# Opening of a spectral filter plus gated MLP kernel: column 0 in feature halves, first weights on ScalarE's queue, column 1 transposed inside the first up unit

## The chip, the cores and the metric

The kernel runs on one NeuronCore of a Trainium2 chip. The metric is the device time of one execution in microseconds (us); a time given for a kernel is the median of several runs. Traces come from one profiled execution, and times in them are counted from the start of its span.

## The reference

The input x has 2048 rows of 512 features (bfloat16). It is layer-normalized, and two branches of the normalized rows are added to x: a spectral filter (2-D real FFT, product with a complex weight, inverse FFT) and a gated MLP with 1792 hidden features.

```python
def _A_ref(x, w_r, w_i):
    X = rfft2(x.astype(float32), axes=(-2, -1))
    X = X * (w_r + 1j * w_i)
    return irfft2(X, s=(S, D), axes=(-2, -1)).astype(bfloat16)

def _B_ref(x, w_gate, w_up, w_down):
    g = einsum("bsd,df->bsf", x, w_gate)
    u = einsum("bsd,df->bsf", x, w_up)
    h = _gelu(g) * u                      # tanh form of gelu
    return einsum("bsf,fd->bsd", h, w_down)

xn = _layernorm(x, axis=-1)               # eps 1e-5
return x + _A_ref(xn, A_w_r, A_w_i) + _B_ref(xn, B_w_gate, B_w_up, B_w_down)
```

## The kernel before, in words

Row 16·p + c of x lies in partition p, column c. So x is held as 16 columns of 128 rows by 512 features (`x_t`), and "column c" below always means such a block. Each column is normalized into `xn` and transposed into `xnT`, four blocks of 128 features (e = 0 to 3) by rows, because the matmuls contract over features.

The MLP is cut into units. A unit takes n columns and m blocks of 128 hidden features (f): matmuls with `Wg_sb` into the PSUM tile `g_ps`, matmuls with `Wu_sb` into `u_ps`, a GELU on ScalarE from `g_ps` to `ge`, and on VectorE the product of `u_ps` and `ge` into `hT`. `g_ps` and `u_ps` have two buffers each; a GELU frees one of the first, a product one of the second. The first units are small, so that the work can begin when a single column is there: unit 0 is column 0 with f 0 to 3, unit 1 column 1 with f 0 to 3, units 2 and 3 are columns 0 and 1 with f 4 and 5 and with f 6 and 7; the next four take columns 2 and 3, and then come units of four columns and one f. The `todo` list has them in this order. The spectral branch (`forward`, `group`, `inverse`) and the down projection (`down`) fill the rest of the program.

The order on every engine is written out ahead. `opening()` emits the first memsets, the loads and 37 matmuls on zeros (`spin`), which keep TensorE busy until data come. All else is added to a `Plan` as operations with an engine, an assumed occupancy and latency, dependencies, a key and, for what needs a load, an assumed earliest time (`LAND`, `WG_LAND`, `WU_LAND`). `Plan.order()` simulates the engines with these numbers and emits the operations in the order it finds; the chip then keeps that order on each engine, and real waits come from semaphores. A changed assumption can therefore move operations anywhere in the program.

`first_two()` (line 372) plans columns 0 and 1. For column 0: moments on VectorE (L337), aggregate (L340), square root on ScalarE (L392), reciprocal (L397), normalization in two halves of 256 features (L343), four transposes on TensorE (L349), two copies of `tp` into `xnT` on ScalarE (L352), and in between six more spin matmuls (L322). For column 1 the same, with the normalization, the four transposes and the one copy (VectorE) undivided; the transposes stand in the key order after unit 0 and ahead of unit 1. The entry named `table` stands for the change of ScalarE's function table from Sqrt to GELU; it emits nothing, and the load itself is put in by the compiler ahead of the first GELU. `second_two()` plans columns 2 and 3 with their square roots on POOL (`root_eps`), and `later_four()` the others, which are transposed by DMA.

Unit 0 is emitted through `mm_half` (line 488), which runs e = 0, 1 over all four f and then e = 2, 3, so that it may begin with half of `xnT`. All other units use `mm` (line 480), which finishes one f after the other.

The loads are issued in program order by two queues, SyncE (SP) and ScalarE. A load takes one of eight semaphores in turn, and waits for the load that had it before.

Of the kernel before, what the change touches and what calls it, by code (L numbers as in the profile page):

```python
# [10 lines left out]
P = 128  # L11
BF16 = mybir.dt.bfloat16
F32 = mybir.dt.float32
# [4 lines left out]
S = 2048  # L18
D = 512
NC = 16  # L20
NG = 8
NE = 4
# [112 lines left out]
class Plan:  # L135
# [66 lines left out]
def kernel(  # L202
# [11 lines left out]
    nc = tc.nc  # L214
# [5 lines left out]
    x_v = A_x.rearrange("b (p c) d -> p c (b d)", c=NC)  # L220
# [7 lines left out]
    pw = ctx.enter_context(tc.tile_pool(name="pw", bufs=2))  # L228

    x_t = pc.tile([P, NC, D], BF16, name="x_t", tag="x_t")  # L230
    CT = pc.tile([P, const_np.shape[1]], BF16, name="CT")
    Wg_sb = pc.tile([P, NE, DF], BF16, name="Wg_sb")
    Wu_sb = pc.tile([P, NE, DF], BF16, name="Wu_sb")
# [19 lines left out]
    def load_x(c0, n, eng=nc.sync):  # L253
        eng.dma_start(out=x_t[:, c0:c0 + n, :], in_=x_v[:, c0:c0 + n, :])

    def load_w(a, b, eng=nc.sync):
        nc.sync.dma_start(out=Wg_sb[:, :, a:b], in_=wg_v[:, :, a:b])
        eng.dma_start(out=Wu_sb[:, :, a:b], in_=wu_v[:, :, a:b])
# [15 lines left out]
    def opening():  # L274
        nc.vector.memset(spin[:], 0.0)
        nc.vector.memset(eps_t[:], EPS)
        nc.vector.memset(minus_half[:], -0.5)
        U = nc.gpsimd
        U.memset(ident_t[:], 1.0)
        U.affine_select(out=ident_t[:], in_=ident_t[:], pattern=[[-1, P]], compare_op=ALU.is_equal, fill=0.0,  # L280
                        base=0, channel_multiplier=1)
        nc.scalar.activation(out=warm[:], in_=eps_t[:], func=AF.Sqrt, bias=eps_t[:], scale=1.0)
        load_x(0, 1)
        load_x(1, 1)
        load_w(Wg_sb, 0, 512, nc.scalar, e=slice(0, 2))
        load_w(Wg_sb, 0, 512, nc.scalar, e=slice(2, 4))
        for e in range(NE):
            load_w(Wu_sb, 0, 512, e=e)
        load_x(2, 2)
        load_w(Wg_sb, 512, 1024)  # L290
        load_w(Wu_sb, 512, 1024)
        load_x(4, 4)
        load_w(Wg_sb, 1024, DF)
        load_w(Wu_sb, 1024, DF)
        load_x(8, 4)
        nc.sync.dma_start(out=RF_t[:], in_=rf_d.rearrange("p (c k) -> p c k", c=NC))
        load_x(12, 4)
        nc.sync.dma_start(out=idx_t[:], in_=nc.inline_tensor(idx_np, name="spec_rows").ap())
        load_consts("F0", "L0")
        load_consts("I0", "M0")  # L300
        for T, w_in in ((TR, A_w_r), (TI, A_w_i)):
            rows = w_in.rearrange("(kb a h g) k -> h kb a (g k)", kb=NC, h=2, a=8)
            Tf = T.rearrange("p j k -> p (j k)")
            for h in range(2):
                nc.sync.dma_start(out=Tf[64 * h:64 * h + 64, W:8 * W], in_=rows[h, :, 0:4, W:8 * W])
        for k in range(37):
            nc.tensor.matmul(sp_ps[:, :P], lhsT=spin[:], rhs=spin[:], start=True, stop=True)  # L307

    LAND = {0: 2.9, 1: 4.5, 2: 7.2, 3: 7.2}
    LAND.update({c: 11.5 if c < 8 else 17.5 if c < 12 else 20.5 for c in range(4, NC)})  # L310
    WG_LAND = [5.0] * 4 + [8.6] * 4 + [13.2] * 6
    WU_LAND = [6.7] * 4 + [10.0] * 4 + [15.2] * 6
    RF_LAND = 19.0

    ident = ident_t[:]
# [23 lines left out]
    def f_mean(c):  # L339
        V.bn_aggr(out=mv[:, c, :], in_=tiles["st", c][:])  # L340

    def f_norm_v(c, o, w):
        V.tensor_scalar(out=xn[:, c, o:o + w], in0=x_t[:, c, o:o + w], scalar1=mv[:, c, 0:1],  # L343
                        scalar2=rstd[:, c:c + 1], op0=ALU.subtract, op1=ALU.mult)

    def f_T(c, e0, n):
        tiles["T", c, e0] = tp = ps.tile([P, n, P], BF16, name="tp", tag="S", bufs=4)
        for e in range(n):
            T_.transpose(tp[:, e], xn[:, c, (e0 + e) * P:(e0 + e + 1) * P], ident)  # L349

    def f_Tc(c, e0, n, copy=V.tensor_copy):
        copy(out=xnT[0][:, e0:e0 + n, c, :], in_=tiles["T", c, e0][:])  # L352
# [14 lines left out]
        U.tensor_tensor(out=b, in0=mv[:, c0:c0 + n, 0], in1=rstd[:, c0:c0 + n], op=ALU.mult)  # L367
        U.tensor_scalar(out=b, in0=b, scalar1=-1.0, scalar2=None, op0=ALU.mult)  # L368

    xn_op, xT_op = {}, {}  # L370

    def first_two():
        o = {}

        def v(k, fn, occ, deps=(), lat=None, t_min=0.0):
            o[k] = add("DVE", occ, fn, [o[d] for d in deps], key=-2000 + len(o), lat=lat, t_min=t_min,
                       after=o.get("last"))
            o["last"] = o[k]

        def T(c, h):  # L380
            o["T", c, h] = add("PE", 0.12, lambda: f_T(c, 2 * h, 2), [o["xn", c, h]], key=-2000 + 2 * c + h,
                               lat=0.36, acq=("S",))

        def xn_(c, h):
            v(("xn", c, h), lambda: f_norm_v(c, 256 * h, 256), 0.27, [("recip", c)], lat=0.4)

        def stats(c):
            v(("stats", c), lambda: f_stats(c), 0.6, t_min=LAND[c], lat=0.7)

        def mean(c):  # L390
            v(("mean", c), lambda: f_mean(c), 0.17, [("stats", c)])
            o["root", c] = add("ACT", 0.31, lambda: A.activation(  # L392
                out=rstd[:, c:c + 1], in_=mv[:, c, 1:2], func=AF.Sqrt, bias=eps_t[:], scale=1.0),
                [o["mean", c]], key=-2000 + c)

        def recip(c):
            v(("recip", c), lambda: V.reciprocal(out=rstd[:, c:c + 1], in_=rstd[:, c:c + 1]), 0.15, [("root", c)])  # L397

        stats(0)
        mean(0)  # L400
        recip(0)
        xn_(0, 0)
        xn_(0, 1)
        stats(1)
        mean(1)
        T(0, 0)
        T(0, 1)
        add("PE", 0.33, spin_on, [o["T", 0, 1]], key=-1500, lat=0.33, after=o["T", 0, 1])
        table = add("ACT", 1.3, lambda: None, [o["root", 1]], key=-1500, lat=1.3)
        xT_op[0, 0], xT_op[0] = (  # L410
            add("ACT", 0.36, lambda h=h: f_Tc(0, 2 * h, 2, A.copy), [o["T", 0, h]], key=-1990 + h, lat=0.48,
                rel=("S",)) for h in range(2))
        recip(1)
        xn_op[0] = o["xn", 0, 1]
        v("xn1", lambda: f_norm_v(1, 0, D), 0.33, [("recip", 1)], lat=0.45)
        t = add("PE", 0.23, lambda: f_T(1, 0, NE), [o["xn1"]], key=-1998, lat=0.45, acq=("S",))
        o["t"] = t
        v("copyt", lambda: f_Tc(1, 0, NE), 0.5, ["t"])
        o["copyt"].rel = ("S",)
        xT_op[1] = o["copyt"]  # L420
        xn_op[1] = o["xn1"]
        return o["copyt"]

    ROOT = 1.1
    chain_end = first_two()
# [39 lines left out]
    def unit(k, c0, n, f0, m=1):  # L465
# [19 lines left out]
                    T_.matmul(b[name][:, f], lhsT=W_[:, e, (f0 + f) * P:(f0 + f + 1) * P], rhs=rhs[:, e, :],  # L485
                              start=(e == 0), stop=(e == NE - 1))

        def mm_half(s, name="g_ps", tag="G", W_=Wg_sb):
            if s == 0:
                b[name] = ps.tile([P, m, w], F32, name=name, tag=tag, bufs=2)  # L490
            for e in (2 * s, 2 * s + 1):
                for f in range(m):
                    T_.matmul(b[name][:, f], lhsT=W_[:, e, (f0 + f) * P:(f0 + f + 1) * P], rhs=rhs[:, e, :],  # L493
                              start=(e + f == 0), stop=(e == NE - 1), skip_group_check=True)
# [12 lines left out]
        def split(name, tag, W_, key, t, h):  # L507
            o = None
            for f in range(0, m, h):
                o = add("PE", occ * h / m, lambda f=f: mm(name, tag, W_, range(f, f + h)), [o] if f else src, key=key,  # L510
                        lat=occ * h / m + 0.3, acq=() if f else (tag,), t_min=t[f0 + f + h - 1])
            return o

        if k == 0:
            g = add("PE", occ / 2, lambda: mm_half(0), [xT_op[0, 0]], key=1000, acq=("G",), t_min=WG_LAND[0])
            g = add("PE", occ / 2, lambda: mm_half(1), [xT_op[0], g], key=1000.1, lat=occ / 2 + 0.3)
            u = add("PE", occ / 2, lambda: mm_half(0, "u_ps", "U", Wu_sb), [g], key=1000.5, acq=("U",), t_min=6.2)
            u = add("PE", occ / 2, lambda: mm_half(1, "u_ps", "U", Wu_sb), [u], key=1000.6, lat=occ / 2 + 0.3,
                    t_min=WU_LAND[0])
        else:  # L520
            g = split("g_ps", "G", Wg_sb, 1000 + k, WG_LAND, m)
            u = split("u_ps", "U", Wu_sb, 1000.5 + k, WU_LAND, (2, m, 1)[k] if k < 3 else m)
        ge = add("ACT", {1: 0.28, 2: 0.36, 4: 0.5}[n * m], f_ge, [g], key=-1000 + k,
                 lat={1: 0.38, 2: 0.48, 4: 0.7}[n * m], acq=("ge",), rel=("G",))
        h = add("DVE", {1: 0.21, 2: 0.34, 4: 0.61}[n * m], f_h, [ge, u], key=-1000 + k, rel=("U", "ge"))
# [354 lines left out]
```

## Time and profile before

| | us |
|---|---|
| median of four runs | 178.89 |
| their lowest and highest | 178.69, 180.44 |
| the profiled execution | 179.09 |
| its span | 177.4 |
| TensorE busy in the span | 172.1 |
| first matmul of unit 0, of unit 1 | 6.07, 9.23 |
| first transpose of columns 2 and 3 | 12.76 |

In lines of the profile, PE is TensorE's matmul side, PEld its weight loads, DVE is VectorE, ACT is ScalarE, POOL is GpSimd, SP is SyncE. A name such as SPq or ACTq is the issue of a DMA by that engine. `L485` is line 485 of the kernel. A bracket at the end of a line tells how long the engine had been idle and what ended it. In a line of waits the numbers are the total, the count and the longest wait.

### The profile page before, as it was taken

Reading aid. Unit: us, or ns where it says so; the run is one execution under the profiler, and the core shown is the slowest. Engines: PE = TensorE matmul, PEld = TensorE weight load, DVE = VectorE, ACT = ScalarE, POOL = GpSimd, SP = SyncE. Lnnn points to the kernel's source line nnn. Section 1 sums busy time; section 2 is a strip of 40 time slices with the busy share of each in tenths; the row PEclk is TensorE's granted clock in tenths of the full one; section 3 lists DMA queues with packets and bytes.
Section 4 is the critical chain, followed back from the end, with each engine's and each line's share of the span. In section 5 each row is a group of like instructions: output and inputs, shape, how many; then the busy total and the mean of one; then the engine's idle time right before and its main releaser. Section 6 shows DMA issues by size and latency. Waiting matters only on the chain.

```text
span 177.4 us, 3114 instructions
## 1 busy us (share of the span) xinstructions
PE 172.1 (97%) x1128; PEld 97.5 (55%) x1145; DVE 115.6 (65%) x253; ACT 96.4 (54%) x172; POOL 17.0 (10%) x38
## 2 busy tenths in 40 slices
PE   7999999999999999999999999999999999999993
PEld 7888845464545554555555545454445444444463
DVE  2488899988333599998799999543526334344333
ACT  4623489798745989799999955453112111211200
POOL 1020360406760000000000000000000000000000
PEclk9999999999999999999999999999999999999999
DMA  5999986543718702121202520200132221221212
GB/s 149 324 368 393 349 168 99 111 91 56 240 33 265 267 4 59 36 53 35 59 10 49 142 72 0 59 0 4 53 95 89 70 81 61 89 86 62 78 44 59
DMA packets 21360, 19.35 MB, mean 109 GB/s; under 512 B 8481, under 2 KB 20001, under 8 KB 21345
## 3 DMA queue, kind: packets, MB, share of 16 engines
q1 hardware_dynamic: 20384, 17.31, 33.8%
q0 software_dynamic: 416, 1.32, 2.6%
q10 hardware_dynamic: 544, 0.52, 1.1%
q8 instruction: 9, 0.15, 0.4%
q14 instruction: 7, 0.05, 0.1%
HBM read 13.38 MB, written 2.10 MB: 87 GB/s over the span
## 4 chain that ended last, share of the span: by engine, by line
PE 97%; issue 1%; DVE 1%
PE u_ps L485 27%; PE y_ps L815 27%; PE g_ps L485 26%; PE sp_ps L307 2%; PE yp L766 2%; PE dp L633 2%; PE gp L736 2%; PE bp L575 2%; PE y_ps L819 2%; PE ep L642 2%; PE g_ps L493 1%; PE tp L349 1%; PE u_ps L493 1%; PE sp_ps L322 0%; DVE xnT L352 0%
## 5 line engine op out<-in xcount | busy, mean ns | idle before, releaser
L485 PE MATMUL u_ps<-xnT,Wu_sb 128*128 128x512 bf16 (+2 forms) x254 | 56.5, 349 | 0.3
L485 PE MATMUL g_ps<-xnT,Wg_sb 128*128 128x512 bf16 (+2 forms) x246 | 55.2, 348 | 0.8 <-DVE xnT L352 0.5
L503 DVE TENSOR_TENSOR hT<-u_ps,ge 128x512 bf16<-128x512 f32 x56 | 38.4, 687 | 18.8 <-PE u_ps L485 15.3
L815 PE MATMUL y_ps<-Wd_sb,hT 128*128 128x512 bf16 (+2 forms) x247 | 50.5, 355 | 0.2
L498 ACT ACTIVATE ge<-g_ps 128x512 bf16<-128x512 f32 x56 | 33.7, 602 | 22.6 <-PE g_ps L485 20.5
L815 PEld LDWEIGHTS <-hT 128*128 128x128 bf16 x252 | 23.2, 98 | 22.4
L485 PEld LDWEIGHTS <-Wu_sb 128*128 128x128 bf16 x256 | 24.0, 98 | 20.9
L485 PEld LDWEIGHTS <-Wg_sb 128*128 128x128 bf16 x256 | 23.8, 98 | 20.5 <-issue 0.6
L772 ACT CAST yf<-yp 128x512 bf16<-128x512 f32 x16 | 9.3, 586 | 40.5 <-PE yp L766 40.5
L822 DVE TENSOR_TENSOR y_sb<-y_ps,y_sb 128x512 bf16<-128x512 f32 (+2 forms) x18 | 11.1, 631 | 30.1 <-PE y_ps L819 30.1
L647 ACT CAST E<-ep 64x512 bf16<-64x512 f32 x32 | 18.5, 579 | 1.3 <-PE ep L642 0.8
L337 DVE BATCH_NORM_STATS2 stats<-x_t 128x6 f32<-128x512 bf16 x16 | 10.5, 675 | 2.8 <-DMA x_t<-in_A_x_dram 2.8
L447 ACT ACTIVATE xn<-x_t,nb,rstd 128x512 bf16<-128x512 bf16 x12 | 9.5, 814 | 1.8 <-POOL nb L368 1.7
L545 ACT CAST Gs<-gp 128x512 bf16<-128x512 f32 x16 | 9.0, 593 | 1.0 <-PE gp L736 0.9
L545 ACT CAST ds<-dp 128x512 bf16<-128x512 f32 x16 | 9.0, 598 | 0.6 <-PE dp L633 0.5
L545 ACT CAST Bs<-bp 128x512 bf16<-128x512 f32 x16 | 8.6, 609 | 0.5 <-PE bp L575 0.5
L778 DVE TENSOR_TENSOR lv<-yf 128x512 bf16<-128x512 bf16 x16 | 6.1, 420 | 1.5 <-ACT yf L772 0.9
L766 PEld LDWEIGHTS <-Gs 128*128 128x128 bf16 x64 | 4.8, 98 | 3.5
L785 DVE TENSOR_TENSOR yt<-lv 128x512 bf16<-128x512 bf16 x16 | 6.1, 420 | 0.3
L766 PE MATMUL yp<-CT,Gs 128*128 128x128 bf16 x64 | 6.0, 219 | 0.1
L819 PE MATMUL y_ps<-yt,RI_t 128*128 128x512 bf16 (+2 forms) x18 | 6.1, 355 | 0.0
L736 PEld LDWEIGHTS <-F 128*128 128x128 bf16 x64 | 4.5, 98 | 2.6
(67 smaller groups left out, 124.4 us busy)
## 6 DMA issues: line engine op xcount, KB each, us to landing
F<-F SPq DMA_DIRECT2D x32, 64.0 KB, 2.0
y_sb<-in_A_x_dram SPq DMA_DIRECT2D x16, 128.0 KB, 2.1
out_dram<-y_sb SPq DMA_DIRECT2D x15, 128.0 KB, 1.7
Wd_sb<-in_B_w_down_dram SPq DMA_DIRECT2D x1, 1792.0 KB, 7.8
x_t<-in_A_x_dram SPq DMA_DIRECT2D x3, 512.0 KB, 11.0
Wg_sb<-in_B_w_gate_dram SPq DMA_DIRECT2D x1, 768.0 KB, 9.1
Wu_sb<-in_B_w_up_dram SPq DMA_DIRECT2D x1, 768.0 KB, 10.7
Wg_sb<-in_B_w_gate_dram ACTq DMA_DIRECT2D x2, 256.0 KB, 3.9
```

Of the source, the lines that this page charges most:

```text
L337: V.bn_stats(out=st[:], in_=x_t[:, c, :])
L447: xn_op[c] = add("ACT", 0.72, lambda c=c: A.activation(out=xn[:, c, :], in_=x_t[:, c, :], func=AF.Identity, bias=nb[:, c:c + 1], scale=rst ...
L485: T_.matmul(b[name][:, f], lhsT=W_[:, e, (f0 + f) * P:(f0 + f + 1) * P], rhs=rhs[:, e, :], start=(e == 0), stop=(e == NE - 1))
L498: A.activation(out=b["ge"][:], in_=b["g_ps"][:], func=AF.Gelu_apprx_tanh)
L503: V.tensor_tensor(out=hT_of(sb, f0, m, o, w), in0=b["u_ps"][:], in1=b["ge"][:], op=ALU.mult)
L545: A.copy(out=o, in_=i)
L647: A.copy(out=b["E"][64 * h:64 * h + 64, r], in_=b["ep", h][64 * r:64 * r + 64])
L766: T_.matmul(t[:, q], lhsT=late["G"][:, q, c0 + j], rhs=IQ[q], start=(q == 0), stop=(q == 3), skip_group_check=True)
L772: A.copy(out=b["yf"][:, j], in_=b[j][:])
L815: T_.matmul(b[o][:], lhsT=hT_of(sb, f, 1, cl * P, P)[:, 0], rhs=Wd_sb[:, f, o:o + w], start=(f == 0), stop=False)
L819: T_.matmul(b[o][:], lhsT=late["RI"][:, c, :], rhs=late["yt"][:, c, o:o + w], start=False, stop=True)
L822: V.tensor_tensor(out=b["y"][:, o:o + w], in0=b[o][:], in1=b["y"][:, o:o + w], op=ALU.add)
```

## The change

Seven things are edited, all of them in the opening.

- Column 0 is loaded by two DMAs of 256 features each, and its moments are taken in two halves (`f_stats_half`), which the same aggregate joins.
- The first blocks of `Wu_sb` (hidden features 0 to 511) are loaded by two DMAs instead of four, on ScalarE's queue behind those of `Wg_sb`; so is the load of columns 2 and 3.
- POOL copies one element of column 0 into the place of `Wg_sb` that the load of features 512 to 1023 overwrites. That load, and with it the rest of SyncE's queue, is held until column 0 has landed.
- Columns 12 to 15 are loaded by two DMAs of two columns.
- The assumed landing times change.
- Column 1's four transposes are planned as two pairs, after the first quarter (e = 0) of unit 0's up matmuls and ahead of the second. The pair's two copies go to VectorE and to ScalarE.
- Unit 1's gate matmuls run in two halves over e, like those of unit 0; `mm_half` becomes `mm_part` with a range of e.

```diff
-        load_x(0, 1)
+        for o in (0, 256):
+            nc.sync.dma_start(out=x_t[:, 0, o:o + 256], in_=x_v[:, 0, o:o + 256])
         load_x(1, 1)
-        load_w(Wg_sb, 0, 512, nc.scalar, e=slice(0, 2))
-        load_w(Wg_sb, 0, 512, nc.scalar, e=slice(2, 4))
-        for e in range(NE):
-            load_w(Wu_sb, 0, 512, e=e)
-        load_x(2, 2)
+        for T in (Wg_sb, Wu_sb):
+            for e in (0, 2):
+                load_w(T, 0, 512, nc.scalar, e=slice(e, e + 2))
+        load_x(2, 2, nc.scalar)
+        U.tensor_copy(out=Wg_sb[0:1, 0, 512:513], in_=x_t[0:1, 0, D - 1:D])
         load_w(Wg_sb, 512, 1024)
...
-        load_x(12, 4)
+        load_x(12, 2)
+        load_x(14, 2)
...
-    LAND = {0: 2.9, 1: 4.5, 2: 7.2, 3: 7.2}
+    LAND = {0: 2.65, 1: 4.6, 2: 7.2, 3: 7.2}
...
-    WU_LAND = [6.7] * 4 + [10.0] * 4 + [15.2] * 6
+    WU_LAND = [6.4] * 4 + [10.2] * 4 + [15.2] * 6
...
+    def f_stats_half(c, h):
+        if h == 0:
+            tiles["st", c] = pw.tile([P, 2, V.BN_STATS_DIM], F32, name="stats2", bufs=1)
+        V.bn_stats(out=tiles["st", c][:, h, :], in_=x_t[:, c, 256 * h:256 * h + 256])
...
-        stats(0)
+        v("half", lambda: f_stats_half(0, 0), 0.3, t_min=2.5, lat=0.3)
+        v(("stats", 0), lambda: f_stats_half(0, 1), 0.3, t_min=LAND[0], lat=0.4)
...
-        t = add("PE", 0.23, lambda: f_T(1, 0, NE), [o["xn1"]], key=-1998, lat=0.45, acq=("S",))
-        o["t"] = t
-        v("copyt", lambda: f_Tc(1, 0, NE), 0.5, ["t"])
...
+        o["t", 0] = add("PE", 0.12, lambda: f_T(1, 0, 2), [o["xn1"]], key=1000.54, lat=0.3, acq=("S",))
+        o["t", 1] = add("PE", 0.12, lambda: f_T(1, 2, 2), [o["xn1"]], key=1000.55, lat=0.3, acq=("S",),
+                        after=o["t", 0])
+        between.update(o)
+        v("copyt0", lambda: f_Tc(1, 0, 2), 0.25, [("t", 0)], lat=0.4)
+        o["copyt1"] = add("ACT", 0.4, lambda: f_Tc(1, 2, 2, A.copy), [o["t", 1], table], key=-1400)
...
-        def mm_half(s, name="g_ps", tag="G", W_=Wg_sb):
+        def mm_part(e0, e1, name="g_ps", tag="G", W_=Wg_sb):
...
-            u = add("PE", occ / 2, lambda: mm_half(0, "u_ps", "U", Wu_sb), [g], key=1000.5, acq=("U",), t_min=6.2)
-            u = add("PE", occ / 2, lambda: mm_half(1, "u_ps", "U", Wu_sb), [u], key=1000.6, lat=occ / 2 + 0.3,
-                    t_min=WU_LAND[0])
+            u = add("PE", occ / 4, lambda: mm_part(0, 1, *up), [g], key=1000.5, acq=("U",))
+            between["t", 0].deps.append(u)
+            u = add("PE", occ / 4, lambda: mm_part(1, 2, *up), [u, between["t", 1]], key=1000.6)
+            u = add("PE", occ / 2, lambda: mm_part(2, NE, *up), [u], key=1000.7, lat=occ / 2 + 0.3, t_min=WU_LAND[0])
+        elif k == 1:
+            g = add("PE", occ / 2, lambda: mm_part(0, 2), [xT_op[1, 0]], key=1001, acq=("G",))
+            g = add("PE", occ / 2, lambda: mm_part(2, NE), [*src, g], key=1001.3, lat=occ / 2 + 0.3)
```

In the compiled order of the changed kernel TensorE runs unit 0's gate matmuls, four up matmuls, column 1's four transposes, twelve up matmuls, and then unit 1. ScalarE has the five load issues ahead of column 0's root, and column 1's copy ahead of the load of the GELU table. VectorE and ScalarE keep their order up to the first units; from there on the planner places moments, evacuations and the spectral matmuls somewhat differently, mostly by one or two units.

More of the change, by code (lines that the diff above doesn't have):

```diff
@@ L368, in bias @@
         U.tensor_scalar(out=b, in0=b, scalar1=-1.0, scalar2=None, op0=ALU.mult)
-    xn_op, xT_op = {}, {}
+    xn_op, xT_op, between = {}, {}, {}
     def first_two():
@@ L415, in first_two @@
         v("xn1", lambda: f_norm_v(1, 0, D), 0.33, [("recip", 1)], lat=0.45)
-        t = add("PE", 0.23, lambda: f_T(1, 0, NE), [o["xn1"]], key=-1998, lat=0.45, acq=("S",))
-        o["t"] = t
-        v("copyt", lambda: f_Tc(1, 0, NE), 0.5, ["t"])
-        o["copyt"].rel = ("S",)
-        xT_op[1] = o["copyt"]
+        o["t", 0] = add("PE", 0.12, lambda: f_T(1, 0, 2), [o["xn1"]], key=1000.54, lat=0.3, acq=("S",))
[4 more added lines that the diff above has]
+        o["copyt1"] = add("ACT", 0.4, lambda: f_Tc(1, 2, 2, A.copy), [o["t", 1], table], key=-1400)
+        o["copyt0"].rel = o["copyt1"].rel = ("S",)
+        xT_op[1, 0] = o["copyt0"]
+        xT_op[1] = o["copyt1"]
         xn_op[1] = o["xn1"]
-        return o["copyt"]
+        return o["copyt0"]
     ROOT = 1.1
@@ L486, in mm @@
                               start=(e == 0), stop=(e == NE - 1))
-        def mm_half(s, name="g_ps", tag="G", W_=Wg_sb):
-            if s == 0:
+        def mm_part(e0, e1, name="g_ps", tag="G", W_=Wg_sb):
+            if e0 == 0:
                 b[name] = ps.tile([P, m, w], F32, name=name, tag=tag, bufs=2)
-            for e in (2 * s, 2 * s + 1):
+            for e in range(e0, e1):
                 for f in range(m):
@@ L512, in split @@
             return o
+        up = "u_ps", "U", Wu_sb
         if k == 0:
-            g = add("PE", occ / 2, lambda: mm_half(0), [xT_op[0, 0]], key=1000, acq=("G",), t_min=WG_LAND[0])
-            g = add("PE", occ / 2, lambda: mm_half(1), [xT_op[0], g], key=1000.1, lat=occ / 2 + 0.3)
-            u = add("PE", occ / 2, lambda: mm_half(0, "u_ps", "U", Wu_sb), [g], key=1000.5, acq=("U",), t_min=6.2)
-            u = add("PE", occ / 2, lambda: mm_half(1, "u_ps", "U", Wu_sb), [u], key=1000.6, lat=occ / 2 + 0.3,
-                    t_min=WU_LAND[0])
+            g = add("PE", occ / 2, lambda: mm_part(0, 2), [xT_op[0, 0]], key=1000, acq=("G",), t_min=WG_LAND[0])
+            g = add("PE", occ / 2, lambda: mm_part(2, NE), [xT_op[0], g], key=1000.1, lat=occ / 2 + 0.3)
+            u = add("PE", occ / 4, lambda: mm_part(0, 1, *up), [g], key=1000.5, acq=("U",))
[5 more added lines that the diff above has]
+            g = add("PE", occ / 2, lambda: mm_part(2, NE), [*src, g], key=1001.3, lat=occ / 2 + 0.3)
+            u = split(*up, 1001.5, WU_LAND, m)
         else:
             g = split("g_ps", "G", Wg_sb, 1000 + k, WG_LAND, m)
-            u = split("u_ps", "U", Wu_sb, 1000.5 + k, WU_LAND, (2, m, 1)[k] if k < 3 else m)
+            u = split("u_ps", "U", Wu_sb, 1000.5 + k, WU_LAND, 1 if k == 2 else m)
         ge = add("ACT", {1: 0.28, 2: 0.36, 4: 0.5}[n * m], f_ge, [g], key=-1000 + k,
```

## The prediction

> **What bounds the kernel now.** I read the page first (busy shares), then the waits of TensorE alone, then busy time by stage, then the order of time over the first 14 us.
>
> The page's part 1, busy time per engine, and the waits of TensorE over the whole span:
>
> ```profile
> PE 172.1 (97%) x1128; PEld 97.5 (55%) x1145; DVE 115.6 (65%) x253; ACT 96.4 (54%) x172; POOL 17.0 (10%) x38
> ...
> PE sp_ps L307 <- DVE minus_half L277: 1.1, 1, 1.1
> PE g_ps L485 <- DVE xnT L352: 0.5, 1, 0.5
> ```
>
> TensorE is the bound; it waits twice: before its first instruction, and once for the transposed column 1. By stage, TensorE alone (stretch, length, busy, granted clock, DMA share, GB/s):
>
> ```profile
> 22.00:40.00 18.00, 17.84 (x115) 1.00 0.65 119
> ...
> 100.00:120.00 20.00, 19.90 (x116) 1.00 0.19 49
> ...
> 174.00:177.40 3.40, 0.61 (x11) 1.00 0.27 77
> ```
>
> From 22 us to 174 us it lacks 0.1 to 0.2 us per 20 us, which is nothing, and the 2.8 us at the end are the last add and store, untouched. So everything is decided before 14 us. The timeline (start, length, engine, line, operation, idle before and its releaser):
>
> ```profile
> 1.05 3.87 PEld L307 LDWEIGHTS <-spin 128*128 128x128 bf16 x37 [1.05 <-DVE minus_half L277]
> 3.11 0.69 DVE L337 BATCH_NORM_STATS2 stats<-x_t 128x6 f32<-128x512 bf16 x1 [2.10 <-DMA x_t<-in_A_x_dram]
> 4.06 0.29 ACT L392 ACTIVATE rstd<-mv,eps_t 128x1 f32<-128x1 f32 x1 [1.67 <-DVE mv L340]
> 4.61 0.39 SPq L270 DMA_DIRECT2D Wg_sb<-in_B_w_gate_dram  x1
> 4.98 0.38 PEld L349 LDWEIGHTS <-xn 128*128 128x128 bf16 x4
> 5.43 0.85 PE L322 MATMUL sp_ps<-x_t,spin 128*128 128x128 bf16 x6
> 6.07 1.53 PE L493 MATMUL g_ps<-xnT,Wg_sb 128*128 128x128 bf16 x16
> 6.35 1.28 ACT L498 ACT_TABLE_LOAD   x1
> 6.56 0.41 DVE L343 TENSOR_SCALAR xn<-x_t,mv,rstd 128x512 bf16<-128x512 bf16 x1
> 7.44 1.06 PE L493 MATMUL u_ps<-xnT,Wu_sb 128*128 128x128 bf16 x16
> 8.33 0.39 PE L349 MATMUL tp<-ident_t,xn 128*128 128x128 bf16 x4
> 8.76 0.42 DVE L352 COPY xnT<-tp 128x512 bf16<-128x512 bf16 x1 [1.78 <-PE tp L349]
> 9.10 1.28 DVE L337 BATCH_NORM_STATS2 stats<-x_t 128x6 f32<-128x512 bf16 x2
> 9.23 1.05 PE L485 MATMUL g_ps<-xnT,Wg_sb 128*128 128x128 bf16 x16 [0.52 <-DVE xnT L352]
> 10.51 1.48 DVE L503 TENSOR_TENSOR hT<-u_ps,ge 128x512 bf16<-128x512 f32 x2
> 11.90 0.73 DVE L343 TENSOR_SCALAR xn<-x_t,mv,rstd 128x512 bf16<-128x512 bf16 x2
> 12.76 0.61 PE L349 MATMUL tp<-ident_t,xn 128*128 128x128 bf16 x8
> ```
>
> Three things are to be seen. The spin matmuls' weight loads run to 4.92 (1.05 + 3.87), only 0.06 before column 0's transposes, so column 0 has hardly room to come earlier. The hole: four transposes at the warm pace (16 u matmuls from 7.44 to 8.33, 0.056 each) end at 8.55, and unit 1 starts at 9.23, a hole of 0.68 (0.52 in the page's modelled ends). And columns 2 and 3 reach TensorE at 12.76, just behind their normalization (11.90 + 0.73 = 12.63).
>
> **What the Trainium skill says.** "DMA: Bandwidth & Descriptors", section "Queues, rings and completion order": SyncE and ScalarE each own a ring on the same 16 DMA engines, and an engine takes turns between its rings packet by packet. The trace agrees: Wg's second half, issued on ScalarE's queue at 1.55, landed 4.4 later at 5.95, while SyncE's queue moved about as many bytes (x columns 0 and 1 and a first quarter or two of Wu). The same page, "Issuing engines are not separate DMA queues": another issuer saves issue time only. The trace bears it out: the DMA share is 1.0 to 1.1 from 3.6 us on. "ScalarE: Activation LUTs", "What ACT_TABLE_LOAD costs": about 1283 ns for any set; the trace has 1.28. "TensorE: Matmul & The Clock Gate", Part 1: half rate until a busy window of about 3.4 us, by time and not by count; here weight loads are 0.105 apart at the start (3.87 over 37) and 0.056 from about 7 us.
>
> **The change, part by part.** All against the profiled execution: span 177.4, time 179.09, so 1.69 outside the span, which the change doesn't touch. It stands 0.20 above the median of 178.89; I carry the difference to the median.
>
> *Column 0 in halves.* Its load was issued at 0.80 and landed 2.3 later at 3.10; moments took 0.69, to 3.80. Now the second half is a second issue one pitch later (0.80 to 1.24). It lands between 3.2 (half the bytes save 0.3) and 3.6 (nothing saved); I take 3.4. Half the moments cost 0.35 (half of 0.69) to 0.45 (with a fixed part); I take 0.4. End 3.8: no gain, -0.2 to +0.2. Even a gain of 0.2 is cut by the spins that end at 4.92: the second pair of transposes could come about 0.1 earlier, and at half clock that is worth 0.05 at the end. Taken as 0. Column 1 is issued one pitch (0.47) later, landing near 5.0 instead of 4.53; DVE reaches it at 5.10 anyway.
>
> *Five issues on ScalarE instead of two.* 0.98 / 2 = 0.49 each from 1.06: they end at 3.5, and column 0's root is due at 4.06. Hidden by 0.55. If that cover goes (a stalled issue), every further tenth moves column 0.
>
> *POOL copy as a gate.* The one such row, a 1x1 copy on POOL (L597), took 0.70. From 3.4 the bulk load Wg 512:1024 is issued at about 4.2 (4.61 before), Wu 512:1024 at 4.7 (5.71), x 4 to 7 at 5.15 (6.22). Behind the waiting copy on POOL stands only the root of columns 2 and 3, due at 10.68. On SyncE all later loads wait behind the gated one, yet go earlier than before.
>
> *Two rings at once.* Before, all that the first units need (1.57 MB) stood ahead of the bulk in order; x 2-3 landed at 3.60 + 4.1 = 7.7. Now Wu's second half and x 2-3 are last on ScalarE's ring and share with the bulk from its first byte, about 1.1 after its issue (column 0: issue 0.80, bytes from 1.9), so from 5.3. Adding the GB/s of 0.4 us stretches, 1.0 MB has moved by 5.3, of which 0.74 MB on that ring; 0.57 MB remain. At half of 390 GB/s until 6.4 (0.21 MB) and half of 280 after: 0.10 MB of Wu by 7.15, landing perhaps 0.5 later, when the u matmuls want it at 8.1; x 2-3 (0.26 MB) by 8.5 (with a larger share for its 2 KB rows) to 9.0, landing 9.0 to 9.5. I take 9.2. Before, DVE only asked at 9.10.
>
> *Column 1's transposes inside the first u unit.* Column 1 is normalized at 6.97 (7.2 if late), the first four u matmuls end at 7.66, the transposes at 7.9. Half copies: VectorE from 8.0, at most 0.42, ScalarE 0.37 (as the column 0 copies): both done by 8.4. Unit 1 begins at 8.55 with halves of its own. The hole closes: -0.68.
>
> *The table load that follows.* The planner has the GELU table loaded before the new ScalarE copy; the compiled order has the copy first. So the load moves from 6.35 to 8.4, ends at 9.7, the first GELU runs at 9.7 to 10.3 (7.64 before). Unit 2's g matmuls, now due at 10.35 instead of 11.02, wait for that buffer: 0.1. Unit 2's u, due at 11.3, needs the first product hT.
>
> *What is late next.* VectorE's order is moments 2, 3 (1.28), two aggregates (0.30), hT twice (1.48), normalization 2, 3 (0.73). From a landing L this gives L + 0.05 + 1.28 + 0.25 + 1.45 + 0.75 = L + 3.8 for the last normalization, and 0.25 for its transposes and the sequel: L + 4.05. Before, unit 3 began at 13.21. With L = 9.2 it begins at 13.25. If L is under 8.8, the first GELU at 10.3 is the bound instead: 10.4 + 1.45 + 0.75 + 0.25 = 12.85, a gain of 0.36. So of the 0.68, between none and half survives; most likely 0.0 to 0.2. I take -0.1: 178.8.
>
> *The rest.* x 12-15 as two loads adds one issue (0.47) near 10 us to a queue whose data is used after 20 us. The new plan moves the forward transform's matmuls by about a unit, later ones by up to two; TensorE has no wait there before, and none is expected: 0, at most +0.5.
>
> **Rivals.** *The hole is worth nearly its size.* ScalarE's ring drains early, x 2-3 lands before 8.8, or the clock rises at a better moment: 0.36 to 0.6 gained, 178.4. For it: Wg's bytes flow early in both. Against: the DMA is saturated from 3.6 on, and the bulk is issued sooner.
>
> *Slower: x 2-3 lands late.* Place: VectorE's in-order queue, where hT of units 0 and 1 stands behind the moments of columns 2 and 3, and unit 2's u matmuls wait for hT. It decides from L = 9.16 (9.16 + 4.05 = 13.21), and each us later costs a us. With L = 10 the time is 178.89 + 0.85 = 179.7; beyond 1% only if L passes 11. For it: ring sharing and the low 250 to 300 GB/s from 6.4 to 9.6. Against: the 2 KB rows.
>
> *The later order goes wrong*, a stall in the re-planned middle: +0.5 to +2, 179.5 to 181. Nothing in the profile speaks for it.
>
> **How the numbers follow.** Wash, 0.50; gain, 0.25; late columns 2-3, 0.19; later order, 0.06. The likeliest gives 178.8. The range goes from 178.2 (the full hole) to 179.9 (L near 10.2). About 1%, 1.8 us, is what a measurement of this kernel can tell from no change: faster by that has no source in a hole of 0.68 (0.02); slower needs L over 11 or the later order (0.06).
>
> **What would show it.** Right: no wait of unit 1 for xnT; the table load near 8.4; moments of column 2 begin near 9.2 on a DMA wait; unit 3 near 13.2. The column 0 step is wrong if its moments end before 3.6; the ring step if column 2's moments begin before 8.8 or after 9.6. The whole is wrong if TensorE shows a new wait after 14 us, or if the start of unit 3 moves by more than 0.6.

## The result and the profile after

The changed kernel takes 179.75 us (median of 42 runs, 178.99 to 180.93), the kernel before 179.05 us (63 runs, 178.42 to 180.44). The ratio is 1.0039, with a 95% interval of [1.0026, 1.0052]: slower by 0.7 us, where 0.1 us of gain was forecast. The profiled execution of the changed kernel took 179.56, with a span of 177.5.

Two plain sums come before the trace. Time minus span is 1.97 in the median over the runs of the changed kernel and 1.71 for the kernel before: about 0.25 of the loss lies outside the span. And the spans themselves are of two kinds. Of 44 executions of the changed kernel, 26 have spans of 177.0 to 177.9 (median 177.2) and 18 of 178.2 to 179.0 (median 178.7). For the kernel before, spans are on record from the runs beside the experiments below: 118 executions, all between 176.7 and 178.2, and only two of them at 178.2. So a good execution of the changed kernel has no longer a span than before, and two in five cost about 1.5 us more. (The kernel before is not quite free of this: three of its 63 times lie above 180.1.) The median over both groups is 177.75, against 177.3 to 177.4: the rest of the loss, about 0.45.

The profiled execution is of the first group; no execution of the second was profiled for this kernel. Its waits of TensorE (line, tile, what was waited for; total, count, longest):

```profile
PE sp_ps L309 <- DVE minus_half L277: 1.1, 1, 1.1
PE tp L356 <- DVE xn L350: 0.8, 1, 0.8
PE u_ps L497 <- DMA Wu_sb<-in_B_w_up_dram: 0.2, 1, 0.2
```

The wait of unit 1 for `xnT` (0.5 before) is gone. Two have come: column 0's transposes now wait for column 0, and unit 2's u matmuls for the weights of hidden features 512 to 1023. The timeline of the changed kernel (start, length, engine, line, operation, idle before it):

```profile
2.67 0.43 DVE L347 BATCH_NORM_STATS2 stats<-x_t 128x6 f32<-128x256 bf16 x1 [1.65 <-DMA x_t<-in_A_x_dram]
3.12 0.49 ACTq L266 DMA_DIRECT2D x_t<-in_A_x_dram  x1
4.33 0.43 DVE L347 BATCH_NORM_STATS2 stats<-x_t 128x6 f32<-128x256 bf16 x1 [1.24 <-DMA x_t<-in_A_x_dram]
4.36 0.18 POOL L290 COPY Wg_sb<-x_t 1x1 bf16<-1x1 bf16 x1 [2.99 <-DMA x_t<-in_A_x_dram]
4.57 0.39 SPq L270 DMA_DIRECT2D Wg_sb<-in_B_w_gate_dram  x1
...
5.96 0.54 PE L356 MATMUL tp<-ident_t,xn 128*128 128x128 bf16 x4 [0.79 <-DVE xn L350]
...
6.71 1.05 PE L505 MATMUL g_ps<-xnT,Wg_sb 128*128 128x128 bf16 x16
...
7.60 0.39 PE L505 MATMUL u_ps<-xnT,Wu_sb 128*128 128x128 bf16 x4
...
8.01 0.40 PE L356 MATMUL tp<-ident_t,xn 128*128 128x128 bf16 x4
...
8.54 1.28 DVE L339 BATCH_NORM_STATS2 stats<-x_t 128x6 f32<-128x512 bf16 x2
8.84 1.28 ACT L510 ACT_TABLE_LOAD   x1
...
8.92 1.06 PE L505 MATMUL g_ps<-xnT,Wg_sb 128*128 128x128 bf16 x16
...
12.01 1.05 PE L497 MATMUL u_ps<-xnT,Wu_sb 128*128 128x256 bf16 x8 [0.19 <-DMA Wu_sb<-in_B_w_up_dram]
...
13.34 1.04 PE L497 MATMUL g_ps<-xnT,Wg_sb 128*128 128x256 bf16 x8
```

The first half of column 0 is there at 2.67. The second is there only at 4.33, where the whole column had been there at 3.11. Its moments end at 4.76 (3.80 before), and the transposes begin at 5.96 (4.98): column 0 is one us late. The spins still end at 4.91, so TensorE's weight loads stand idle for 1.05. In this execution that costs little: the 16 gate matmuls of unit 0 run at full pace from the start (1.05, where they took 1.53 before, the first of them at the slow pace of the spins), and its u matmuls begin at 7.60, only 0.16 later than before. Column 1's transposes at 8.01 fit into unit 0, unit 1 follows at 8.92 without a hole (9.23 before), columns 2 and 3 arrive early enough that VectorE starts on them at 8.54 with no wait for a load, and still unit 3 begins 0.13 later than before (13.34 against 13.21). Unit 2's u matmuls took the gain: at 12.01 against 11.89 in the kernel before. What they wait for is the last line here, from the DMA issues of the first 20 us (queue, count, size, median time from issue to landing):

```profile
x_t<-in_A_x_dram ACTq DMA_DIRECT2D x1, 256.0 KB, 5.1
...
Wu_sb<-in_B_w_up_dram SPq DMA_DIRECT2D x1, 512.0 KB, 7.0
```

Columns 2 and 3, issued at 3.12, landed at 8.2. The u weights, issued at 5.00, landed at 12.0. In the kernel before they were issued at 5.71 and took 5.8, to 11.5; unit 2's first weight load came at 11.78. The two lines of the kernel before:

```profile
11.78 0.86 PEld L485 LDWEIGHTS <-Wu_sb 128*128 128x128 bf16 x8
...
Wu_sb<-in_B_w_up_dram SPq DMA_DIRECT2D x1, 512.0 KB, 5.8
```

So before the change they had about 0.3 us to spare.

Later TensorE meets no new wait. All engines, in the stretch from 22 to 40 us (length; busy time of PE, PEld, DVE, ACT and POOL; granted clock; DMA share; GB/s):

```profile
22.00:40.00 18.00, 17.84 (x107) 9.20 (x108) 16.89 (x34) 15.85 (x27) 4.72 (x8) 1.00 0.55 105
```

TensorE is 17.84 us busy of 18, as before. The last add starts at 174.77 (174.65 before), and 2.7 us follow it in both.

### The profile page after: what moved, and what is told of

Read it like the earlier page. It is cut to its first block, busy times and chain, and to the rows that moved or that the text cites. A ratio compares the mean times of both kernels' runs of the same rounds, so it can differ in the third digit from the quotient of the medians.

```text
span 177.5 us, 3118 instructions
## 1 busy us (share of the span) xinstructions
PE 171.7 (97%) x1127; PEld 96.6 (54%) x1145; DVE 115.7 (65%) x254; ACT 96.6 (54%) x173; POOL 17.4 (10%) x39
## 4 chain that ended last, share of the span: by engine, by line
PE 91%; DMA 6%; issue 1%; SPq 0%; DVE 0%; POOL 0%
PE y_ps L833 27%; PE u_ps L497 26%; PE g_ps L497 26%; DMA Wu_sb<-in_B_w_up_dram 4%; PE gp L754 2%; PE yp L784 2%; PE dp L651 2%; PE bp L593 2%; PE y_ps L837 2%; PE ep L660 2%; DMA x_t<-in_A_x_dram 2%; PE tp L356 0%; SPq L270 0%; SPq L284 0%; DVE y_sb L840 0%
## 5 line engine op out<-in xcount | busy, mean ns | idle before, releaser
L497 PE MATMUL u_ps<-xnT,Wu_sb 128*128 128x512 bf16 (+2 forms) x247 | 55.6, 348 | 0.6 <-DMA Wu_sb<-in_B_w_up_dram 0.2
L497 PE MATMUL g_ps<-xnT,Wg_sb 128*128 128x512 bf16 (+1 forms) x237 | 55.0, 357 | 0.2
L497 PEld LDWEIGHTS <-Wg_sb 128*128 128x128 bf16 x240 | 23.0, 98 | 20.6
L339 DVE BATCH_NORM_STATS2 stats<-x_t 128x6 f32<-128x512 bf16 x15 | 9.7, 671 | 0.0
L660 PE MATMUL ep<-ds,CT 128*128 128x512 bf16 x16 | 5.9, 379 | 0.0
```

Of the source, the lines that this page charges most:

```text
L339: V.bn_stats(out=st[:], in_=x_t[:, c, :])
L660: T_.matmul(t[:], lhsT=cc("L" if g + h else "L0"), rhs=b["ds", h][:], start=True, stop=True)
```

## The experiments

The theory after the result: column 0 in halves lands late; the idle TensorE then misses, in some executions, the moment at which its clock rises. The rivals: the slower group comes from the weights or from the re-planned order; and for the 0.25 outside the span, from the copy on POOL, from a split load or from ScalarE's issues. A ratio below is to the kernel before, with runs on the same chip. Each kernel was also profiled once.

**More spins in the changed kernel** (`e1_spin47`). Nothing else differs: the lateness of column 0 stays, and TensorE works longer before it idles.

```diff
-        for k in range(37):
+        for k in range(47):
```

> The changed kernel with 47 spin matmuls instead of 37, so that TensorE has no idle time between 4.9 us and column 0's transposes near 6.0. Clock theory: the changed kernel's times form two groups (about 179.1 and 180.6 us), because an idle TensorE in that stretch delays the rise of its clock in part of the executions; without the idle time the upper group is gone and the median is near 179.1, ratio to before 1.000 to 1.002. Rival, a late load alone: column 0 still lands at 4.3, nothing that follows moves, the two groups stay and the ratio is 1.004 as for the changed kernel.

Measured: 179.30 against 179.02, ratio 1.0019 [1.0009, 1.0028]. The 22 spans lie between 177.1 and 178.1: the upper group is gone, with column 0's transposes in its profile even later (6.37). The timeline of its profile, from 4 us on: the last spins, the transposes and unit 0's gate weight loads:

```profile
3.91 1.38 PEld L309 LDWEIGHTS <-spin 128*128 128x128 bf16 x19
...
6.37 0.37 PEld L356 LDWEIGHTS <-xn 128*128 128x128 bf16 x4 [1.08 <-DVE xn L350]
...
7.03 0.96 PEld L505 LDWEIGHTS <-Wg_sb 128*128 128x128 bf16 x16
```

The idle stretch is still 1.08, since in this execution the second half came only at 4.74. But the 19 last spins took 0.073 each, where the 37 of the changed kernel took 0.104: the clock rose among them, before the idle stretch, and was still up at 7.03, where 16 weight loads took 0.060 each. So one us of idle time after the rise did no harm; what costs, in some executions, is idle time before it. (The good execution above idled before the rise as well, and got by.) What is left of the loss, 0.28, is the part outside the span (1.96 here, 1.71 before). The order and the weights are the same as in the changed kernel, so neither makes the upper group.

**Fewer spins in the kernel before** (`e5_spin28`). The reverse test: nothing of the change, but idle time ahead of the transposes.

```diff
-        for k in range(37):
+        for k in range(28):
```

> The kernel before with 28 spin matmuls instead of 37: they end near 3.98, so TensorE idles about 1 us before column 0's transposes at 4.98; loads and all other work as before. Clock theory: that idle time alone makes two groups of times, about 178.9 and 180.3 us, as in the changed kernel; ratio 1.003 to 1.008. Rival, the late load alone matters: nothing that the kernel computes is later, the ratio stays at 1.000 to 1.001 in one group.

Measured: 179.86 against 179.14, ratio 1.0027 [1.0009, 1.0045]. The spans spread into two groups, though the gap between them is narrow: ten of 22 up to 177.9 with a median of 177.1, and twelve from 178.1 with 178.35, where the 48 of the kernel before on the same chip have one at 178.2 and all others below 178.1. The ratio is just under the range that was expected. The profiled execution fell in the upper one (178.3):

```profile
5.51 0.65 PE L349 MATMUL tp<-ident_t,xn 128*128 128x128 bf16 x4 [1.29 <-DVE xn L343]
...
6.49 1.75 PEld L493 LDWEIGHTS <-Wg_sb 128*128 128x128 bf16 x16
...
10.16 1.05 PE L485 MATMUL g_ps<-xnT,Wg_sb 128*128 128x128 bf16 x16 [0.51 <-DVE xnT L352]
```

Sixteen weight loads take 1.75 us, 0.109 each: the pace of the spins. In the run with 47 spins they took 0.96, 0.060 each. The spins had ended at 3.94, and column 0 came at 3.63. With an idle stretch of 1.3 us (of the matmuls) to 1.6 us (of the weight loads) before the rise, and no other edit, the clock stays low through the gate matmuls of unit 0, and unit 1 starts at 10.16 where it had started at 9.23. Of these 0.93, 0.52 is column 0's later landing in this execution (3.63 against 3.11) and the other 0.41 the low clock. Late landings alone do not make the group: the kernel before has the same loads.

**Only the halves, in the kernel before** (`e3_halves`).

```diff
-        load_x(0, 1)
+        for o in (0, 256):
+            nc.sync.dma_start(out=x_t[:, 0, o:o + 256], in_=x_v[:, 0, o:o + 256])
...
-        stats(0)
+        v("half", lambda: f_stats_half(0, 0), 0.3, t_min=2.5, lat=0.3)
+        v(("stats", 0), lambda: f_stats_half(0, 1), 0.3, t_min=LAND[0], lat=0.4)
```

> The kernel before with column 0 loaded in two halves and its moments taken in two, nothing else. If the half loads are the cause, the second half lands near 4.3, TensorE idles about 1 us before column 0's transposes, and the times split in two groups: ratio 1.004 to 1.010. Rival, the queues: with four Wu loads on SyncE behind it and two on ScalarE, column 0 is complete by 3.5 and the ratio is 0.999 to 1.002.

Measured: 180.01 against 179.02, ratio 1.0077 [1.0047, 1.0106]; the part outside the span is 1.73. The second half's moments begin at 4.33 again and the transposes at 5.96, as in the changed kernel. Here Wu and columns 2 and 3 are still on SyncE's queue. So the lateness belongs to the halves themselves, and not to what ScalarE's queue was given besides. In this profile the clock is up for unit 0's gate matmuls, unit 3 starts at 13.37 (0.16 late), the last add at 175.08 (0.43 late), and the stretch from there to the end of the span is 3.2 instead of 2.7, half a us that column 0 does not explain. Two groups, as expected, can't be told in six executions: five spans lie between 178.2 and 178.7, one at 179.8.

**The changed kernel with column 0 whole** (`e2_whole0`), the edit above undone.

> The changed kernel with column 0 loaded and its moments taken in one piece, all else as changed. If the second half's load (landing 3.1 after its issue) is the cause, column 0 lands near 3.1, TensorE does not wait for it, the upper group of times is gone, and the closed hole of unit 1 shows: ratio 0.996 to 0.999. Rival, the queues: if moving the first weights and columns 2-3 to ScalarE's queue costs the time, the load of Wu 512 to 1023 still lands near 12 and unit 2 waits for it: ratio 1.001 to 1.003 without two groups.

Measured: 180.06 against 179.02, ratio 1.0065 [1.0043, 1.0086]. Both theories missed: the column is back in time and the kernel is slower than the changed one. The profile tells why:

```profile
3.24 0.39 SPq L270 DMA_DIRECT2D Wg_sb<-in_B_w_gate_dram  x1
...
8.19 0.62 PE L503 MATMUL u_ps<-xnT,Wu_sb 128*128 128x128 bf16 x8 [0.64 <-DMA Wu_sb<-in_B_w_up_dram]
...
9.82 1.29 DVE L338 BATCH_NORM_STATS2 stats<-x_t 128x6 f32<-128x512 bf16 x2 [2.28 <-DMA x_t<-in_A_x_dram]
```

The gate waits for column 0. With column 0 early it opens at 3.24 instead of 4.57, the two bulk loads share the DMA engines with the second half of Wu and with columns 2 and 3, and these come at 8.18 and 9.8 instead of 7.5 and 8.2. That is the collision that the prediction feared, here with an earlier gate. In the changed kernel the late column held the gate shut and so protected them.

**Column 0 whole and the gate on column 1** (`e6_whole0_gate1`), to have the early column and the late gate at once.

```diff
-        U.tensor_copy(out=Wg_sb[0:1, 0, 512:513], in_=x_t[0:1, 0, D - 1:D])
+        U.tensor_copy(out=Wg_sb[0:1, 0, 512:513], in_=x_t[0:1, 1, D - 1:D])
```

> The changed kernel with column 0 and its moments in one piece and POOL's gate on column 1 (landing 4.5 to 5.0) instead of column 0 (3.0). Contention theory: what made the whole-column variant slow (1.0065) is that its gate opened at 3.2, so that the bulk loads shared the engines with Wu's second half and columns 2 and 3; with the gate at about 5 the wait of unit 0 for Wu (0.6 to 0.8 us) and the late moments of columns 2 and 3 are gone, ratio 0.999 to 1.002. Rival, ScalarE's queue is slow whatever the bulk does: Wu's second half still lands after 7.8, ratio 1.004 or more. About 0.25 us more outside the span than before is expected in both.

Measured: 179.78 against 179.14, ratio 1.0027 [1.001, 1.0044]. Two lines of its profile:

```profile
4.91 0.39 SPq L270 DMA_DIRECT2D Wg_sb<-in_B_w_gate_dram  x1
...
5.34 0.37 PEld L355 LDWEIGHTS <-xn 128*128 128x128 bf16 x4 [0.43 <-DVE xn L349]
```

The gate opens at 4.9, no wait for Wu is left in unit 0, columns 2 and 3 are there by 8.12, and unit 3 starts at 12.83. So the collision was rightly named. The ratio is still above the range that was expected: 1.95 lies outside the span, and the spans reach from 176.6 to 178.7, 5 of 22 at 178.2 or more. In the profile column 0 landed at 3.47 and TensorE's weight loads stood idle for 0.43, so this kernel too has the idle gap in at least some executions. Its column 0 is whole, so the halves are not the only source of long spans; whether the move of loads to ScalarE's queue delays column 0 was not tried by itself.

**Only the compute part, with the loads of before** (`e4_inner`): column 1's transposes inside unit 0, the pair's two copies, unit 1 in halves; all loads, the column 0 moments and the assumed landing times as in the kernel before.

```diff
-        for o in (0, 256):
-            nc.sync.dma_start(out=x_t[:, 0, o:o + 256], in_=x_v[:, 0, o:o + 256])
+        load_x(0, 1)
...
-        U.tensor_copy(out=Wg_sb[0:1, 0, 512:513], in_=x_t[0:1, 0, D - 1:D])
```

> The loads, the moments and the assumed landing times of the kernel before, with only the compute part of the change: column 1 transposed inside the first up unit, its copies split over VectorE and ScalarE, unit 1's gate matmuls in halves. By the hole of 0.68 us: unit 1 starts at 8.55 instead of 9.23 and 0.0 to 0.6 us are gained, ratio 0.997 to 1.000, one group of times. If the load of Wu 512 to 1023 (landing 11.5) is what unit 2 then waits for, or columns 2 and 3, the gain is under 0.3. Rival: the delayed table load costs more than the hole, ratio 1.001 or more.

Measured: 178.95 against 179.02, ratio 1.0005 [0.9994, 1.0016]: no difference that can be told. Its timeline, TensorE's matmuls and weight loads (PEld):

```profile
8.15 1.06 PE L502 MATMUL g_ps<-xnT,Wg_sb 128*128 128x128 bf16 x16
...
11.32 0.77 PEld L494 LDWEIGHTS <-Wu_sb 128*128 128x128 bf16 x8 [0.55 <-DMA Wu_sb<-in_B_w_up_dram]
...
12.65 1.04 PE L494 MATMUL g_ps<-xnT,Wg_sb 128*128 128x256 bf16 x8
```

The hole is closed, unit 1 starting at 8.15. But 0.40 of its lead over 9.23 is there at unit 0's u matmuls already (7.04 against 7.44), since the clock rose earlier in this execution. Of unit 3's 0.56 (12.65 against 13.21) that leaves 0.16 for the edit: unit 2's u matmuls wait until 11.32, and the line of their weight loads names the weights 512 to 1023 (tried in the next experiment). In the medians even that is hardly there: 0.07, and by the interval no more than 0.1. That is what the closing of the hole, with the later table load and the new copies, is worth with these loads.

**The bulk in quarters** (`e8_inner_split`): the compute part, and features 512 to 1023 in four loads, so that unit 2's weights come first.

```diff
-        load_w(Wg_sb, 512, 1024)
-        load_w(Wu_sb, 512, 1024)
+        for a in (512, 768):
+            load_w(Wg_sb, a, a + 256)
+            load_w(Wu_sb, a, a + 256)
```

> The compute part of the change on the loads of before, with the bulk loads of hidden features 512 to 1023 cut into quarters, Wg and Wu 512 to 767 first, then 768 to 1023. In the compute-only run unit 2 waited about 0.5 us for the whole of Wu 512 to 1023, though it uses 256 features of it. If that wait is why closing the hole gave only 0.0005, it goes, and the ratio is 0.996 to 0.999. Rival, columns 2 and 3 (normalized at 11.2 to 11.9) or the 512-byte rows bound it: ratio 1.000 to 1.003.

Measured: 179.87 against 179.14, ratio 1.0046 [1.003, 1.0062]. The wait of unit 2 is gone, so it was the weights. Unit 3 starts at 11.85, 1.36 earlier than in the kernel before; but 0.98 of that is there at unit 0's u matmuls already (6.46 against 7.44), since the clock rose among the spins in this execution (37 in 3.36, where they took 3.87 before). 0.38 is left for the edits, against 0.16 without the quarters. All of the 1.36 is given back, the last add starting at 174.82 (174.65 before). The first two lines here are the lead, the last two where it begins to go:

```profile
6.46 0.39 PE L503 MATMUL u_ps<-xnT,Wu_sb 128*128 128x128 bf16 x4
...
11.85 1.04 PE L495 MATMUL g_ps<-xnT,Wg_sb 128*128 128x256 bf16 x8
...
20.18 1.29 DVE L338 BATCH_NORM_STATS2 stats<-x_t 128x6 f32<-128x512 bf16 x2 [0.95 <-DMA x_t<-in_A_x_dram]
...
22.11 1.02 PE L495 MATMUL u_ps<-xnT,Wu_sb 128*128 128x512 bf16 x4 [0.50 <-DVE hT L513]
```

VectorE has got ahead of a load of x and waits 0.95 for it; the product `hT` stands behind those moments in its order, and TensorE's u matmuls wait for the buffer that `hT` frees (weight loads idle for 0.78 before 22.12). Another 0.43 goes before 40.49, where TensorE waits for ScalarE. In this execution what came sooner met the next load that did not. The stretch after the last add is 3.2 again, another half a us.

**Copy and split load in the kernel before** (`e7_gate_split`), for the part outside the span.

```diff
         load_x(2, 2)
+        U.tensor_copy(out=Wg_sb[0:1, 0, 512:513], in_=x_t[0:1, 0, D - 1:D])
...
-        load_x(12, 4)
+        load_x(12, 2)
+        load_x(14, 2)
```

> The kernel before with two small parts of the change: POOL's copy as a gate (open at about 3.3, earlier than the load that it holds, 4.6) and columns 12 to 15 in two loads. In the runs so far the time outside the span is 1.65 to 1.75 us where ScalarE issues two loads and 1.9 to 2.05 where it issues five and POOL copies. If the gate or the split load causes it, this kernel shows 1.9 to 2.05 and a ratio of 1.001 to 1.002; if the issues on ScalarE do, it shows 1.65 to 1.75 and a ratio of 0.999 to 1.001.

Measured: 179.96 against 179.14, ratio 1.0045 [1.0027, 1.0063], and 1.96 outside the span. ScalarE issues two loads here, as before, so its issues are not the cause of the part outside. The ratio itself missed (1.002 at most was expected): of the 0.82, 0.25 lies outside the span, and in the profile the stretch after the last add is 3.2 again, although that add starts 0.2 earlier than before (174.45).

**The changed kernel without the copy** (`e9_nogate`).

```diff
-        U.tensor_copy(out=Wg_sb[0:1, 0, 512:513], in_=x_t[0:1, 0, D - 1:D])
```

> The changed kernel without the one-element copy on GpSimd. Theory: the copy itself accounts for the 0.25 us outside the span (1.96 in the changed kernel and in the kernel before with copy and split load, 1.71 before): outside the span back to 1.7. Rival: the load of columns 12 to 15 in two pieces accounts for it: stays at 1.95. Inside the span the theory of the shared DMA engines expects the bulk loads to be issued from about 2.1, the second half of Wu and columns 2 and 3 to land later than 7.5 and 8.2, TensorE to wait for Wu in unit 0, and unit 3 at 13.5 or later (13.34 in the changed kernel). Ratio to the kernel before 1.002 to 1.006 if the copy accounts for the part outside the span, 1.004 to 1.008 if not.

Measured: 1.73 outside the span. The split load is still there, so the copy on POOL is what costs 0.25. Over all runs the division is clean: the five kernels with the copy (the changed one, e1, e2, e6, e7) have medians of 1.95 to 1.97, the kernel before and the six without it (e3, e4, e5, e8, e9, e10) 1.70 to 1.73. The time was a miss: 182.06 against 179.11, ratio 1.0162 [1.0137, 1.0186], far above what both theories gave. Its timeline:

```profile
4.64 0.34 SPq L266 DMA_DIRECT2D x_t<-in_A_x_dram  x1
...
6.28 0.35 ACTq L266 DMA_DIRECT2D x_t<-in_A_x_dram  x1
6.67 0.29 ACT L398 ACTIVATE rstd<-mv,eps_t 128x1 f32<-128x1 f32 x1 [4.29 <-DMA x_t<-in_A_x_dram]
...
8.58 1.75 PEld L504 LDWEIGHTS <-Wg_sb 128*128 128x128 bf16 x16
```

The issue of columns 2 and 3, at 3.12 in the changed kernel, is made only at 6.28, when column 1 has landed (issued at 1.71, 4.5 later). Column 0's root stands behind it on ScalarE, though its moments were ready at 5.3. The loads take eight semaphores in turn, and with the bulk issued from 2.18 the turn has moved; that this is why the issue waits is argued from the order and not tried. A second issue fits it: columns 4 to 7 go at 4.64, as column 0's second half lands (4.65). TensorE is idle for 3 us, and the gate matmuls of unit 0 run at 0.109 per weight load.

**The compute part with 41 spins** (`e10_inner_spin41`), as the best that these runs point to.

```diff
-        for k in range(37):
+        for k in range(41):
```

> The loads of the kernel before, the changed computation of units 0 and 1, and 41 spin matmuls instead of 37, so that no execution has an idle gap ahead of column 0's transposes. Theory of the clock: spans in one group, 176.8 to 177.6, ratio to the kernel before 0.996 to 0.999. Rival: the four further spins (0.42 us of half-clock work) delay column 0's transposes by as much and give the whole back: ratio 1.000 to 1.003.

Measured: 178.91 against 179.11, ratio 0.999 [0.9979, 1.0001], spans of 176.8 to 178.2, a little beyond the 177.6 that was expected at most. It is faster than the changed kernel; that it is faster than the kernel before can't be told.

## Why the prediction was wrong, step by step

The forecast was a gain of 0.1 and the result a loss of 0.70. About 0.45 of the difference comes from executions with a late rise of the clock, 0.25 from outside the span, and the last 0.1 is the gain that another load took.

- *Column 0 in halves* is the step that failed first. "I take 3.4" was 4.33, and "End 3.8: no gain" was 4.76. What was "Taken as 0" made column 0 one us late. The bound of 3.2 to 3.6 took "nothing saved" as the worst: that the second half could land later than the whole had landed was left out. The second half landed 3.1 after its issue at about 1.24, the whole column 2.3 after its own. (Column 1, put near 5.0, landed at 5.7; VectorE came to it at 6.08, so that cost nothing.) The Trainium skill, "DMA: Bandwidth & Descriptors", section "Queues, rings and completion order", has the DMA engines take turns between the two queues, and Wg's halves, issued at 1.06 and 1.56, are on the other; a small load that comes second would then wait for its share. That fits, but no run took Wg away, so it is argued.
- The cost of idle time ahead of those transposes is the term that the sum did not have. The prediction read the spins' end at 4.92, 0.06 ahead of the transposes, and drew from it only that column 0 could not come earlier. Its price for a shift of these transposes was a half: 0.1 us at half clock is worth 0.05 at the end. e1 and e5 show another: most executions lose either about nothing or 1.25 to 1.5 us. e1 takes 0.42 of the 0.70 away by spins alone. That the halves are the only source of the idle time is not shown (e6). The page that the prediction cited for the clock, "TensorE: Matmul & The Clock Gate", says in Part 1 that the window is free-running, so that the moment of the rise depends on where in it the work falls. Two groups of otherwise equal executions agree with that, and so do the spins, of which 37 took from 3.36 (e8) to 3.87 (e4) with the same instructions; the window's place in an execution was not measured.
- "1.69 outside the span, which the change doesn't touch": it is 1.97, by the copy on POOL (e7 and e9); why a copy costs there stays open.
- *Five issues on ScalarE* held: they ended at 3.6, and the root at 5.04 waited for the aggregate. e9 shows what the named cover was worth: one stalled issue there, and the kernel lost 3 us.
- *POOL copy as a gate*: 0.18 and not 0.70, and opened at 4.57 and not 4.2, since it waited for the late half.
- *Two rings at once* was wrong in size. Columns 2 and 3 landed at 8.2, not at 9.2, and their moments began before the 8.8 named as the mark of a mistake. The bulk was issued 0.4 later than assumed, and from 6 to 8 us 358 GB/s flowed in all, where 280 had been counted for after 6.4. The reading behind it was wrong: "the DMA share is 1.0 to 1.1 from 3.6 us on" holds to 6.4, and from there to 9.6 the share in the kernel before is 0.83 to 1.00 with 256 to 290 GB/s, so the engines were not full and there was room. With an early gate (e2) the landing was 9.8: the mechanism is there.
- *Column 1's transposes inside the first u unit* and *the table load that follows* were right: no wait of unit 1, load at 8.84 (8.4 said), first GELU at 10.13 (9.7 to 10.3).
- *What is late next* named the wrong load. With columns 2 and 3 at 8.2 it gave 12.85 for unit 3, and 13.34 was measured, because unit 2's u matmuls wait for Wu 512 to 1023. Its landing at 11.5 with a first use at 11.78 was in the trace of before and was not read. e4 shows the closed hole to be worth a tenth of a us at most with these loads, and e8 that the wait goes with earlier weights, but that in its profile the lead is lost later. That unit 3 began near the 13.2 that was named as a sign of being right is luck: another load held it.
- *The rest* was right: no new wait after 14 us.

None of the three rivals was what happened. The slower one put the loss on columns 2 and 3; that its 179.7 is nearly the time that was measured is luck. And 1% was no measure of what can be told from no change: with 42 and 63 runs the interval is 0.13% to either side.

## What to carry to other kernels

Where warm-up work ends just ahead of the first real work, price a late first load twice: by its delay, and by the clock that may rise later if TensorE idles before it has risen; a few more spins were a cheap insurance here (e1). When a hole is to be closed, list every load that the next units want, with its landing and first use in the trace of before: with the loads as they are, the least slack bounds the gain. And look at time minus span beside the span, since an edit can add there.

## What the runs showed of the hardware

- Idle time of TensorE (1.05 and 1.6 us in the profiles), begun before its clock had risen, went with executions in two groups 1.25 to 1.5 us apart, the slower of 18 in 44 (changed kernel) and 12 in 22 (e5). Ten more spins, and none of 22 executions was above 178.1 (e1).
- The clock did not rise at one moment: the same 37 spins took 3.36 (e8) to 3.87 us (e4).
- After 3 us of idleness (e9) the clock was low again: 0.109 per weight load, although the 37 spins before had run at 0.092 on the mean, part of them fast.
- A one-element copy on POOL that took 0.18 inside the span added 0.25 outside it, in every kernel that had it.
- Half a column landed later (4.33 to 4.74 in four profiles) than a whole one (2.95 to 3.63 in eight) when it was the second of two loads.
- In three kernels (e3, e7, e8) the stretch from the last add to the end of the span took 3.2 instead of 2.7. They issue one or two loads more than the kernel before, and the others as many or one fewer. That the eight semaphores then fall differently on the last stores is a guess; it was not tried.
